# Rests of the first weights: from a subtraction on GpSimd and VectorE to two matmuls and a ScalarE eviction

## The chip, the cores and the metric

The kernel runs on one core of a Trainium2 chip. The metric is device time in microseconds (us) of one execution of the whole program. Five engines work from queues of their own: TensorE (PE in the profile; PEld is its weight load), VectorE (DVE), ScalarE (ACT), GpSimd (POOL) and SyncE (SP), which here only issues DMAs. TensorE writes to PSUM, eight banks of 128 x 512 float32; VectorE and ScalarE read PSUM, GpSimd does not in this kernel.

## The reference

Three steps on 4 x 768 tokens of 8 heads x 48 = 384 features, all float32:

```
for t in range(768):                        # linear attention with decay, state 48 x 48 per head
    cur   = u*k[t] outer v[t]
    y[t]  = r[t] @ (state + cur)
    state = w[t]*state + k[t] outer v[t]
h   = max(y @ w1, y @ w2, y @ w3)           # 384 -> 768, three products, elementwise maximum
x   = h @ w_out                             # 768 -> 384
g   = x @ w_in;  g = g - tanh(g)            # 384 -> 2048
out = g @ w_out2                            # 2048 -> 384
```

The weights arrive as float64 bits, two int32 words per number. The kernel turns each into float32 itself and then splits it into a high part `hi` (the number rounded to the fp32r kind that TensorE multiplies in one pass) and a rest `lo = g - hi`, also fp32r.

## The kernel before

**Products.** Every product of the two feed-forward layers is made of three fp32r matmuls (`mm3`, lines 438 to 441): weight `hi` by activation `hi` (L439), weight `lo` by activation `hi` (L440), weight `hi` by activation `lo` (L441), summed in one PSUM bank of 512 columns.

**Stages.** The 24 chunks of 128 tokens are taken in six groups of four. A prologue computes the attention of chunks 0 to 3. Then comes one pass per group: 18 slots (six blocks `f` of 128 hidden features, three products each, nine matmuls per slot), then three output tiles `d` of 18 matmuls with `WOh`/`WOl`. During the slots of a group the attention of the next group is woven in: `advance(slot)` (L606) issues its steps, twenty for four chunks. After group 5 comes the second layer (`h_unit`, `o_unit`), which the change leaves alone.

**Conversion of the first weights.** The weights of the first layer are 24 units of 128 x 384: units 0 to 17 are the slots' weights in order, units 18 to 23 those of the output tiles, two for each. `w1_unit` (L482) converts one with `conv` (L431): ScalarE takes the high word (L64), VectorE makes the float32 bits in four instructions (L70 to L73), ScalarE rounds to `hi` (L435), and GpSimd subtracts to `lo` (L436); for the four units in `LO_DVE` VectorE subtracts. `g` lies in a ring `cv` of five tiles. Each unit's raw bits are loaded on SyncE's queue eight units ahead.

**When units are issued.** The prologue issues 0, 1, 3 and 4 of them after chunks 0, 1, 2 and 3 (`PRO`), so units 0 to 7. In group 0, `w1_upto(slot + 4 + max(0, slot - 8))` at the end of a slot issues unit 8 after slot 5, one unit after each of slots 6, 7 and 8, and two after each of slots 9 to 14. So unit 23 is issued after slot 14.

**Banks.** `mm` is a ring over banks 0 to 3 that runs on through all groups. A slot's bank is read out by ScalarE (L624, first product) or VectorE (L626, maximum with the others); an output tile's by ScalarE (L650). Banks 4 and 5 hold attention scores (with 0 and 1 in the prologue), 6 and 7 attention outputs and small sums. `h_unit` takes banks 0 and 1 in turn.

**Order.** Tiles and semaphores are the framework's: it takes the program's order as priority and lays down one fixed order per engine. So instructions of two units, or of a slot and the attention, stand interleaved on an engine, and on the chip each engine runs its list strictly as laid down.

Of the kernel before, what the change touches and what calls it, by code (L numbers as in the profile page):

```python
# [10 lines left out]
F32R = mybir.dt.float32r  # L11
# [4 lines left out]
ALU = mybir.AluOpType  # L16
# [3 lines left out]
P = 128  # L20
# [13 lines left out]
EARLY_B = 6  # L34
BONUS_DVE = [0, 1, 2, 4]
VALS_DVE = [5]
LO_DVE = [12, 15, 18, 21]
EARLY_R = [0, 5]
W2A = 12
MM_BANKS = [0, 1, 2, 3]  # L40
# [8 lines left out]
UN = KT * P  # L49
# [13 lines left out]
def abs_f64(act, raw, out):  # L63
    act.activation(out, raw[:, 1::2].bitcast(F32), AF.Abs)  # L64


def bits_f64(dve, raw, out):
    oi = out.bitcast(I32)
    high, low = raw[:, 1::2], raw[:, 0::2]
    dve.tensor_scalar(out, out, bits_f32(LO_BITS), bits_f32(HI_BITS), ALU.max, ALU.min)  # L70
    dve.tensor_scalar(oi, oi, 3, 0x3FFFFFFF, ALU.logical_shift_left, ALU.bitwise_and)  # L71
    dve.scalar_tensor_tensor(oi, high, -0x40000000, oi, ALU.bitwise_and, ALU.bitwise_or)  # L72
    dve.scalar_tensor_tensor(oi, low, 29, oi, ALU.logical_shift_right, ALU.bitwise_or)  # L73
# [16 lines left out]
def main_path(ctx, tc, wT, rkT, w0, rk0, nat, vpad, uT, ub, wA, wo1, wi2, wo2, outT, count):  # L90
    nc = tc.nc
    pe, act, dve, pool, sp = nc.tensor, nc.scalar, nc.vector, nc.gpsimd, nc.sync

    def pool_(name, side="left"):
        return tc.tile_pool(name=name, bufs=1, side=side, reuse_waits="tile")

    const = ctx.enter_context(pool_("const"))
# [11 lines left out]
    bank = [pm.tile([P, 512], F32, name=f"bank{i}") for i in range(8)]  # L109
# [9 lines left out]
    mm = Ring([bank[i] for i in MM_BANKS])  # L119
    scb = Ring([bank[4], bank[5], bank[0], bank[1]])  # L120
    yab, dsb = bank[6], bank[7]

    ident = const.tile([P, P], F32, name="ident")
    dmask = const.tile([P, C], U8, name="dmask")
    ubt = const.tile([P, DM], F32, name="ubt")
    sq = const.tile([P, 2 * NCH], F32, name="sq")
# [37 lines left out]
    def ys(d, g):  # L164
        c = g * 512
        return Y[:, d, c:c + 512] if c < YA else Yb[0][:, d, c - YA:c - YA + 512]
# [207 lines left out]
    def att_steps(c, col):  # L374
        n = c + 1 if c + 1 < NCH else None
        st = {}

        def k0():
            scores(c, st)
            masked(c, st)  # L380
            if n and n < EARLY_B:
                bonus(n)
            if n:
                scans(n)

        def k1():
            if c < EARLY:
                key_turn_pe(c)
            if c >= EARLY_B:
                diagonal(c)  # L390
            if n:
                decays(n)
                if n >= EARLY_B:
                    bonus(n)
                squares(n)

        def k2():
            state_mm(c)
            state_add(c)
            if n:  # L400
                if n >= EARLY:
                    key_turn(n)
                    key_order(n)
                state_decay(n)

        def k3():
            if n:
                bonus_sum(n)

        def k4():  # L410
            outputs(c)
            outputs_out(c, col)
            if n and n < EARLY_B:
                bonus_vals(n)
            load_next(c)

        return [k0, k1, k2, k3, k4]

    def in_range():

        dve.tensor_scalar(sq, sq, 1.0, None, ALU.is_lt)
        dve.tensor_reduce(okp, sq, AX.X, ALU.min)
        pe.matmul(dsb[0:1, 0:1], okp, ones, start=True, stop=True)
        dve.tensor_copy(count, dsb[0:1, 0:1])


    def w1_upto(n):
        while w1n < min(n, 24):
            w1_unit()

    def conv(raw, hi, lo, eng=pool):  # L431
        g = cv()
        abs_f64(act, raw, g)
        bits_f64(dve, raw, g)
        act.copy(hi, g)  # L435
        eng.tensor_tensor(lo, g, hi, ALU.subtract)  # L436

    def mm3(bk, wh, wl, ah, al, first, last):
        pe.matmul(bk, wh, ah, start=first, stop=False)  # L439
# [11 lines left out]
    def warm(n):  # L451

        for _ in range(n):
            pe.matmul(bank[3], zeros[:, 0:P], zeros, start=True, stop=True)

    zeros = xs[:, KT - 1, 256:512].bitcast(BF16)
    pool.memset(zeros, 0.0)
# [9 lines left out]
    act.activation(okp, ones, AF.Square)  # L467
    make_identity(nc, ident)
    pool.tensor_copy(dmask, ident)

    Yi = Y.rearrange("p a b -> p (a b)").bitcast(I32)
    w1raw = [wA[:, i // 3, i % 3 * UN:(i % 3 + 1) * UN] for i in range(3 * F1)]
    w1raw += [wo1[:, i * UN:(i + 1) * UN] for i in range(2 * KT)]

    def w1_load(i):
        sp.dma_start(Yi[:, (i % SLOTS) * 2 * UN:(i % SLOTS + 1) * 2 * UN], w1raw[i].bitcast(I32))

    WAf = [t.rearrange("p f j k m -> p (f j k m)") for t in (WAh, WAl)]
    WOf = [t.rearrange("p d f m -> p (d f m)") for t in (WOh, WOl)]
    w1n = 0  # L480

    def w1_unit():  # L482
        nonlocal w1n
        i = w1n
        w1n += 1
        o = i % SLOTS * 2 * UN
        t, q = (WAf, i) if i < 3 * F1 else (WOf, i - 3 * F1)
        conv(Yi[:, o:o + 2 * UN], t[0][:, q * UN:(q + 1) * UN], t[1][:, q * UN:(q + 1) * UN], dve if i in LO_DVE else pool)
        if i + SLOTS < len(w1raw):
            w1_load(i + SLOTS)  # L490

# [53 lines left out]
    def w2_pump():  # L545
        while free and fetch:
            kind, f = fetch.pop(0)
            staged[kind, f] = free.pop(0)
            sp.dma_start(staged[kind, f], (wi2, wo2)[kind][:, f].bitcast(I32))

    def w2_queue(units):
        todo.extend(units)
        fetch.extend(units)
        w2_pump()
# [23 lines left out]

    c0 = 0
    for g, gn in enumerate(GROUPS):  # L580
        n = gn * C
        lastg = g == len(GROUPS) - 1
        nchunks = [] if lastg else list(range(c0 + gn, c0 + gn + GROUPS[g + 1]))
        steps = [s for i, c in enumerate(nchunks) for s in att_steps(c, i * C)]
        nslots = 3 * F1
        if g == len(GROUPS) - 2:
            def w2_open():
                nonlocal W2a
                in_range()
                p_att.close()  # L590
                p_third.close()
                yb = ctx.enter_context(pool_("yb", "right"))
                Yb.append(yb.tile([P, KT, NT - YA], F32, name="Yb"))
                w2p = ctx.enter_context(pool_("w2p", "right"))
                W2a = [w2p.tile([P, W2A, UN], F32R, name=f"W2{x}a") for x in "hl"]
                free.extend(w2p.tile([P, 2 * UN], I32, name=f"w2st{i}") for i in range(2))
                w2_queue([(0, f) for f in range(W2A)])

            steps += [w2_open, None] + [w2_step] * 6
        if lastg:  # L600
            free.extend([xsi[:, 0:2 * UN], xsi[:, 2 * UN:4 * UN]])
            w2_pump()
            steps = [w2_step] * W2A
        done = 0

        def advance(slot):  # L606
            nonlocal done
            want = min(len(steps), -(-len(steps) * (slot + 1) // nslots))
            while done < want:
                if steps[done]:  # L610
                    steps[done]()
                done += 1
            if g == 0:
                w1_upto(slot + 1 + LEAD + max(0, slot - 8))

        slot = 0
        for f in range(F1):
            for j in range(3):
                bk = mm()
                for k in range(KT):  # L620
                    mm3(bk[:, 0:n], WAh[:, f, j, k], WAl[:, f, j, k], xh[:, k, 0:n], xl[:, k, 0:n], k == 0, k == KT - 1)
                if j == 0:
                    t = tmp()
                    act.copy(t[:, 0:n], bk[:, 0:n])  # L624
                else:
                    dve.tensor_tensor(t[:, 0:n], bk[:, 0:n], t[:, 0:n], ALU.max)  # L626
                if j == 2:
                    act.copy(hh[:, f, 0:n], t[:, 0:n])  # L628
                    (dve if f == F1 - 1 else pool).tensor_tensor(hl[:, f, 0:n], t[:, 0:n], hh[:, f, 0:n], ALU.subtract)  # L629
                advance(slot)  # L630
                slot += 1
        if lastg:
            assert not todo
            p_wA.close()
            wo2p = ctx.enter_context(pool_("wo2p"))
            WO2 = [wo2p.tile([P, F2, UN], F32R, name=f"WO2{x}") for x in "hl"]
            units = [(1, f) for f in range(F2)]
            for i, f in enumerate(range(W2A, F2)):
                units.insert(3 * i + 4, (0, f))
            w2_queue(units)  # L640
        for d in range(KT):
            bk = mm()
            for f in range(F1):
                mm3(bk[:, 0:n], WOh[:, d, f], WOl[:, d, f], hh[:, f, 0:n], hl[:, f, 0:n], f == 0, f == F1 - 1)
            if lastg:
                y_split(0, d)
                w2_step()
            elif d == 0:
                x_split(GROUPS[g + 1] * C)
            act.copy(ys(d, g), bk[:, 0:n])  # L650
        c0 += gn
# [238 lines left out]
```

## Time and profile before

| | |
|---|---|
| median of 3 runs | 881.76 us (880.70 to 886.29) |
| profiled execution | 882.44 us, of which the span of its instructions is 880.7 us |
| TensorE (PE) busy | 839.4 us (95% of the span) |
| VectorE (DVE) busy | 514.6 us (58%) |
| ScalarE (ACT) busy | 335.8 us (38%) |
| GpSimd (POOL) busy | 211.3 us (24%) |
| mean granted TensorE clock | 0.977 of full speed |

Times in the profile count from the span's start. Busy shares of the whole span are means over stages: the prologue (to 55 us), group 0 (to 147 us), groups 1 to 5 (to 463 us) and the second layer each have their own limit. A matmul's printed duration overlaps the next one's, so the pace of matmuls is read from start to start.

### The profile page before, as it was taken

To read this page: it belongs to the slowest core of one execution; us is meant where nothing else is said; L and a number is where in the kernel's file an instruction comes from. 1 tells how busy PE (TensorE), PEld (TensorE's weight loads), DVE (VectorE), ACT (ScalarE), POOL (GpSimd) and SP (SyncE) were. 2 spreads that over 40 slices of the span, in tenths; PEclk is the share of its full clock that TensorE was granted. 3 is DMA by queue.
4 is the path that set the end of the run, shared out by engine and by line. 5 is a ranking of instruction groups with operands and counts; after the bars stand their busy time and mean duration, and the time that the engine had idled before them with its cause. 6 is when DMAs were issued, how large, how long until landed. Compare 5 with 4: busy or idle time off the path is not lost.

```text
span 880.7 us, 12116 instructions
## 1 busy us (share of the span) xinstructions
PE 839.4 (95%) x4546; PEld 663.7 (75%) x4546; DVE 514.6 (58%) x823; ACT 335.8 (38%) x657; POOL 211.3 (24%) x214
## 2 busy tenths in 40 slices
PE   7789498999999999999998999999999999999996
PEld 5768376777777777788876688888888888888885
DVE  8989976774664764738989734334334334333332
ACT  4644434243234243335455433224223224222332
POOL 6665543542343442420253300000000000000000
PEclk8979799999999999999999999999999999999999
DMA  8744353354244253315534100000000000001001
GB/s 265 220 140 123 90 150 87 106 151 118 68 114 137 80 155 106 86 33 154 142 100 131 36 1 36 0 1 37 1 0 36 1 1 36 1 1 36 0 1 39
DMA packets 40561, 66.48 MB, mean 75 GB/s; under 512 B 6256, under 2 KB 21360, under 8 KB 40496
## 3 DMA queue, kind: packets, MB, share of 16 engines
q1 hardware_dynamic: 40496, 65.64, 25.2%
q8 instruction: 37, 0.61, 0.3%
q14 instruction: 28, 0.23, 0.1%
HBM read 53.23 MB, written 8.65 MB: 70 GB/s over the span
## 4 chain that ended last, share of the span: by engine, by line
PE 82%; DVE 10%; DMA 2%; issue 2%; POOL 1%; SPq 1%; ACT 1%; DVEq 0%; ACTq 0%; POOLq 0%
PE bank L439 26%; PE bank L441 25%; PE bank L440 25%; PE bank L347 3%; DVE cv L72 2%; PE bank L278 2%; DVE cv L73 2%; DMA Y<-in_wA 1%; DVE cv L71 1%; PE bank L311 1%; DVE cv L70 1%; DVE fwd L204 1%; DVE suf L202 0%; DMA rk<-in_rkT 0%; DVE hl L670 0%
## 5 line engine op out<-in xcount | busy, mean ns | idle before, releaser
L668 DVE TENSOR_TENSOR tmp<-bank,tmp 128x512 f32<-128x512 f32 x96 | 66.3, 691 | 174.6 <-ACT tmp L667 174.6
L439 PE MATMUL bank<-xh,WAh 128*128 128x512 f32 x324 | 135.5, 418 | 0.0
L441 PE MATMUL bank<-xl,WAh 128*128 128x512 f32 x324 | 130.1, 402 | 0.8 <-DVE xl L367 0.8
L440 PE MATMUL bank<-xh,WAl 128*128 128x512 f32 x324 | 129.8, 401 | 0.0
L667 ACT ACTIVATE tmp<-bank 128x512 f32<-128x512 f32 x96 | 57.4, 598 | 183.0 <-PE bank L441 183.0
L439 PE MATMUL bank<-hh,WO2h 128*128 128x512 f32 x288 | 114.2, 396 | 1.5 <-ACT hh L669 1.4
L441 PE MATMUL bank<-hl,WO2h 128*128 128x512 f32 x288 | 114.3, 397 | 0.4 <-DVE hl L670 0.3
L440 PE MATMUL bank<-hh,WO2l 128*128 128x512 f32 x288 | 113.7, 395 | 0.0
L670 DVE TENSOR_TENSOR hl<-tmp,hh 128x512 fp32r<-128x512 f32 x96 | 66.4, 692 | 58.9 <-PE bank L441 46.8
L669 ACT CAST hh<-tmp 128x512 fp32r<-128x512 f32 x96 | 59.7, 621 | 72.8 <-DVE tmp L668 72.7
L439 PEld LDWEIGHTS bank<-xh,WAh 128*128 128x128 f32 x324 | 61.8, 191 | 18.4 <-issue 2.4
L441 PEld LDWEIGHTS bank<-xl,WAh 128*128 128x128 f32 x324 | 61.8, 191 | 16.5 <-DVE xl L367 1.2
L629 POOL TENSOR_TENSOR hl<-tmp,hh 128x512 fp32r<-128x512 f32 x30 | 46.5, 1550 | 106.5 <-ACT hh L628 106.5
L440 PEld LDWEIGHTS bank<-xh,WAl 128*128 128x128 f32 x324 | 62.1, 192 | 12.7
L441 PEld LDWEIGHTS bank<-hl,WO2h 128*128 128x128 f32 x288 | 54.1, 188 | 15.7 <-DVE hl L670 3.0
L439 PEld LDWEIGHTS bank<-hh,WO2h 128*128 128x128 f32 x288 | 54.1, 188 | 15.6 <-ACT hh L669 3.3
L440 PEld LDWEIGHTS bank<-hh,WO2l 128*128 128x128 f32 x288 | 54.1, 188 | 12.7
L626 DVE TENSOR_TENSOR tmp<-bank,tmp 128x512 f32<-128x512 f32 x72 | 49.0, 680 | 18.6 <-PE bank L441 14.5
L283 DVE COPY_PREDICATED P<-dmask,sd 128x512 f32<-128x512 uint8 x36 | 32.8, 950 | 45.6 <-POOL P L295 45.6
L628 ACT CAST hh<-tmp 128x512 fp32r<-128x512 f32 x36 | 22.4, 621 | 88.2 <-DVE tmp L626 85.3
L439 PE MATMUL bank<-xh,W2ha 128*128 128x512 f32 x108 | 43.3, 401 | 2.8 <-ACT Yb L650 2.8
L439 PE MATMUL bank<-hh,WOh 128*128 128x512 f32 x108 | 43.3, 401 | 0.4 <-ACT hh L628 0.4
(189 smaller groups left out, 1581.8 us busy)
## 6 DMA issues: line engine op xcount, KB each, us to landing
Y<-in_wA SPq DMA_DIRECT2D x18, 384.0 KB, 5.8
nt<-in_nat SPq DMA_DIRECT2D x12, 576.0 KB, 4.9
rk<-in_rkT SPq DMA_DIRECT2D x30, 192.0 KB, 3.4
w2st<-in_wi SPq DMA_DIRECT2D x12, 384.0 KB, 3.6
third<-in_nat SPq DMA_DIRECT2D x7, 576.0 KB, 4.8
kbd<-fwd SPq DMA_DIRECT2D x15, 256.0 KB, 2.1
fwd<-kbd SPq DMA_DIRECT2D x60, 64.0 KB, 2.0
third<-in_rkT SPq DMA_DIRECT2D x16, 192.0 KB, 3.5
```

Of the source, the lines that this page charges most:

```text
L283: dve.copy_predicated(q, dmask[:, None, :].to_broadcast([P, NP, C]), sdt[c % 2][:, j::2, None].to_broadcast([P, NP, C]))
L347: pe.matmul(yab[64 * j:64 * j + HD, p * C:(p + 1) * C], *t(j), start=i == 0, stop=i == len(terms) - 1)
L439: pe.matmul(bk, wh, ah, start=first, stop=False)
L440: pe.matmul(bk, wl, ah, start=False, stop=False)
L441: pe.matmul(bk, wh, al, start=False, stop=last)
L626: dve.tensor_tensor(t[:, 0:n], bk[:, 0:n], t[:, 0:n], ALU.max)
L628: act.copy(hh[:, f, 0:n], t[:, 0:n])
L629: (dve if f == F1 - 1 else pool).tensor_tensor(hl[:, f, 0:n], t[:, 0:n], hh[:, f, 0:n], ALU.subtract)
L667: act.activation(t, bk, AF.Tanh)
L668: dve.tensor_tensor(t, bk, t, ALU.subtract)
L669: act.copy(hh[:, r], t)
L670: dve.tensor_tensor(hl[:, r], t, hh[:, r], ALU.subtract)
```

## The change

The subtraction of the 24 units leaves GpSimd and VectorE. Instead TensorE sums `identity x g` (float32) and `minus identity x hi` (fp32r) into bank 3, and ScalarE copies the sum to `lo`. This is done for unit i when unit i+2 has been issued (`REST_LAG = 2`); the last ones follow unit 23. Bank 3 leaves the `mm` ring in group 0, whose ring is therefore three banks, and the ring is set back to its first bank at the start of every group. The warming matmuls go from bank 3 to bank 2. The conversions of the second layer's weights (`w2_step`) keep their subtractions.

```diff
-LO_DVE = [12, 15, 18, 21]
+REST_LAG = 2
...
+    minus = const.tile([P, P], F32R, name="minus")
...
         act.copy(hi, g)
-        eng.tensor_tensor(lo, g, hi, ALU.subtract)
+        if eng is not pe:
+            eng.tensor_tensor(lo, g, hi, ALU.subtract)
+        return g
+
+    def conv_rest(g, hi, lo):
+
+        pe.matmul(bank[3][:, 0:UN], ident, g, start=True, stop=False)
+        pe.matmul(bank[3][:, 0:UN], minus, hi, start=False, stop=True)
+        act.copy(lo, bank[3][:, 0:UN])
...
-            pe.matmul(bank[3], zeros[:, 0:P], zeros, start=True, stop=True)
+            pe.matmul(bank[2], zeros[:, 0:P], zeros, start=True, stop=True)
...
+    act.mul(minus, ident, -1.0)
...
+    rests = []
...
-        conv(Yi[:, o:o + 2 * UN], t[0][:, q * UN:(q + 1) * UN], t[1][:, q * UN:(q + 1) * UN], dve if i in LO_DVE else pool)
+        hi, lo = (x[:, q * UN:(q + 1) * UN] for x in t)
+        rests.append((conv(Yi[:, o:o + 2 * UN], hi, lo, pe), hi, lo))
+        if len(rests) > REST_LAG or w1n == len(w1raw):
+            conv_rest(*rests.pop(0))
+        if w1n == len(w1raw):
+            while rests:
+                conv_rest(*rests.pop(0))
...
     for g, gn in enumerate(GROUPS):
+        mm.items, mm.i = [bank[i] for i in MM_BANKS[0:3 if g == 0 else 4]], 0
```

## Rows read from the trace of the kernel before

**Rows 1.** Busy time by stretch: us of the stretch, then PE, PEld, DVE, ACT, POOL, clock.

```profile
14.00:55.20 41.20, 32.08 (x268) 28.87 (x268) 39.66 (x62) 24.59 (x66) 26.38 (x28) 0.83 0.74 231
55.20:79.30 24.10, 23.79 (x138) 18.45 (x138) 21.26 (x36) 11.67 (x28) 12.45 (x12) 0.87 0.30 89
79.30:94.90 15.60, 15.59 (x113) 12.19 (x111) 13.70 (x24) 5.33 (x11) 8.97 (x10) 1.00 0.28 87
94.90:107.40 12.50, 0.00 (x0) 0.00 (x0) 12.03 (x19) 6.46 (x13) 6.79 (x7) 0.67 0.33 78
107.40:138.70 31.30, 27.84 (x177) 21.26 (x177) 26.31 (x45) 13.89 (x30) 13.75 (x14) 0.91 0.44 138
138.70:400.00 261.30, 260.29 (x1790) 202.31 (x1791) 158.71 (x240) 97.07 (x200) 101.08 (x109) 1.00 0.37 106
```

**Rows 2.** Timeline of TensorE around its longest wait: start, us, instruction, idle before.

```profile
107.43 0.88 PE L311 MATMUL bank<-nt,kcn 128*48 128x48 f32 x16 [12.54 <-ACT kcn L263]
```

**Rows 3.** Line 436 in three stretches: DVE busy, then POOL busy.

```profile
14.00:55.20 41.20, 0.00 (x0) 10.28 (x7) 0.83 0.74 231
55.20:94.90 39.70, 0.55 (x1) 9.70 (x7) 0.92 0.30 88
94.90:138.70 43.80, 2.26 (x3) 6.54 (x6) 0.84 0.41 121
```

**Rows 4.** Timeline of DVE, ACT and POOL: two conversions, the second beside a GpSimd subtraction.

```profile
99.60 0.56 DVE L72 SCALAR_TENSOR_TENSOR cv<-Y,cv 128x384 int32<-128x384 int32 x1
100.78 0.51 ACT L435 CAST WAh<-cv 128x384 fp32r<-128x384 f32 x1 [1.75 <-DVE cv L73]
101.37 0.99 POOL L436 TENSOR_TENSOR WAl<-cv,WAh 128x384 fp32r<-128x384 f32 x1 [2.92 <-ACT WAh L435]
101.45 1.33 DVE L72 SCALAR_TENSOR_TENSOR cv<-Y,cv 128x384 int32<-128x384 int32 x1
```

**Rows 5.** The same timeline: first and last DVE row lengthened beside line 436.

```profile
17.83 1.98 POOL L436 TENSOR_TENSOR WAl<-cv,WAh 128x384 fp32r<-128x384 f32 x1
18.94 1.43 DVE L216 TENSOR_TENSOR third<-third 128x512 f32<-128x512 f32 x1
...
133.03 1.00 POOL L436 TENSOR_TENSOR WOl<-cv,WOh 128x384 fp32r<-128x384 f32 x1 [4.33 <-ACT WOh L435]
133.20 1.25 DVE L72 SCALAR_TENSOR_TENSOR cv<-Y,cv 128x384 int32<-128x384 int32 x1
```

**Rows 6.** Timeline of TensorE: float32 matmuls of 128 columns, then fp32r at either clock.

```profile
45.88 0.38 PE L334 MATMUL bank<-ident,nt 128*96 128x128 f32 x2
46.10 0.38 PE L335 MATMUL bank<-tmp,nt 128*96 128x128 f32 x2
...
58.10 0.63 PE L440 MATMUL bank<-xh,WAl 128*128 128x512 f32 x1
58.53 0.63 PE L441 MATMUL bank<-xl,WAh 128*128 128x512 f32 x1
...
73.69 0.48 PE L439 MATMUL bank<-xh,WAh 128*128 128x512 f32 x1
74.00 0.39 PE L440 MATMUL bank<-xh,WAl 128*128 128x512 f32 x1
74.24 0.39 PE L441 MATMUL bank<-xl,WAh 128*128 128x512 f32 x1
```

**Rows 7.** Line 352, a ScalarE eviction of 96 x 384: ns min/median/max.

```profile
L352 ACT COPY xs<-bank x5: 462/471/475, 21.2 to 76.9; 96x384 f32<-96x384 f32 x5
```

**Rows 8.** Timeline at the change from group 3 to 4, PE and ACT.

```profile
346.31 0.39 PE L439 MATMUL bank<-xh,WAh 128*128 128x512 f32 x1
...
346.51 0.59 ACT L650 COPY Y<-bank 128x512 f32<-128x512 f32 x1 [1.21 <-PE bank L441]
```

**Rows 9.** Timeline where the second layer starts, PE and ACT.

```profile
468.42 0.80 PE L439 MATMUL bank<-xh,W2ha 128*128 128x512 f32 x1 [2.77 <-ACT Yb L650]
```

## The prediction

> **What bounds the kernel now.** I read the busy times by stretch first, since only the first 139 us hold work that the change touches. From 138.7 us on TensorE is busy 260.29 of 261.30 us [rows 1]: whatever group 0 gains or loses arrives at the end whole. Before that the limit changes hands. To 55.2 us (first matmul of group 0) VectorE is busy 39.66 of 41.20 us: the prologue is VectorE's. From 55.2 to 94.9 TensorE is busy 39.4 of 39.7 us. Then, from 94.9 to 107.4, it does nothing at all while VectorE is busy 12.03 of 12.50 us; and from 107.4 to 138.7 it has 27.84 of 31.30 us, so 3.46 us idle [rows 1]. The timeline shows what the empty stretch is: one attention matmul (L311) waits 12.54 us for ScalarE's copy of the keys, which stands behind roundings that themselves wait for VectorE's conversions [rows 2, 4]; the matmuls of slot 11 stand behind it. So VectorE and TensorE are each the limit for part of the way, and the change takes work from the first and gives work to the second.
>
> **What leaves VectorE and GpSimd.** 20 subtractions of 26.5 us in all go from GpSimd, four of 2.8 us in all from VectorE [rows 3]. GpSimd's own time bounds nothing above; what counts is its neighbour. A conversion's L72 takes 0.56 us alone and 1.33 us when a GpSimd subtraction (0.99 us) starts just before it [rows 4]. In the timeline 18 VectorE rows are lengthened like this beside line 436, the first and last of them shown [rows 5]. Their time over the shortest row of the same form, shared with any other GpSimd instruction they overlap, sums to 10.0 us: 3.9 before 55.2, 4.1 from there to 107.4, 2.1 after. VectorE's own four subtractions are 0.55 us each undisturbed, two before 107.4 and two after. So VectorE is relieved by 3.9 us in the prologue, 5.2 us from there to 107.4, 3.2 us after.
>
> The Trainium skill (GPSIMD Engine Reference, Specifications) says that GpSimd shares its SBUF interfaces with VectorE and contends with VectorE instructions of two SBUF inputs or in a two-port mode. The trace agrees in kind (L72 at 1.33 against 0.56 us). Read at its widest, that all 26.5 us of GpSimd's subtractions come back to VectorE, the rule would take away the 1.9 us of slip below and no more, since TensorE then sets the end: 879 us.
>
> **What TensorE takes on.** A float32 matmul of 128 columns takes 0.22 us from start to start, an fp32r one of 512 columns 0.24 us, the first fp32r after float32 0.31 us [rows 6]. So one rest costs 3 x 0.22 + 0.75 x 0.24 + 0.08 = 0.92 us, an estimate from those rows; no row is of its form. From below, without the change of kind, 0.84; from above, at the lower clock, where the 512 columns take 0.43 us [rows 6], twice the first two terms: 1.7. I take 0.92, since the stretches that matter ran at full clock. By the issue positions unit i's rest follows unit i+2: rests 0 to 5 fall in the prologue, 6 to 13 after slots 5 to 10 (all before 94.9 us), 14 to 23 after slots 11 to 14. The first six are covered by TensorE's idle 9.1 us of the prologue [rows 1] and would cost 5.5 us without it; the next eight meet a TensorE with no room: +7.4 us; the last ten are +9.2 us.
>
> **What ScalarE takes on.** 24 evictions of 384 columns at 0.47 us (the nearest row [rows 7]) make 11.3 us, and one product of 128 columns, earlier. ScalarE is busy 24.59 of 41.20 us in the prologue and half the time later [rows 1], so I cost them at nothing; if each stood in VectorE's chain it would be 2.8 us in the prologue. Behind a late eviction stand the next rounding, attention copies and bank reads. The raw loads on SyncE's queue wait for VectorE's reads as before and are not moved; the renamed warming bank costs nothing, since bank 2 is as empty then as bank 3.
>
> **Less room.** `cv[i]` is now held until rest i, so unit i+5 cannot start before it; and a slot's bank must be read out two slots later instead of three. No row of before shows either wait in this stretch. From below zero; from above 4 us, two undisturbed conversions of 2.0 us (two each of rows like L70 and L72: 2 x 0.35 + 2 x 0.56 = 1.8, and gaps). I take 2.
>
> **The ring set back.** 21 tiles per group on four banks end on bank 0, and the next group now starts on bank 0. At the change from group 3 to 4 the next matmul starts at 346.31 while the last bank is read from 346.51 to 347.10 [rows 8]: on the same bank it would wait 0.8 us. This happens at four changes (groups 1 to 5) and at the second layer's first tile, where already in before the second tile waited 2.77 us for such a read [rows 9]. From below zero (attention scores fill the gap, but for the last two places), from above 4 x 0.8 + 2.8 = 6.0. I take 2.
>
> **The sum.** Group 0 starts 3.5 us earlier (3.9, less what TensorE and ScalarE add). TensorE comes to slot 11's wait at 94.9 - 3.5 + 7.4 = 98.8; VectorE lets go of it at 107.4 - 3.5 - 5.2 = 98.7, with the slip 100.7. So L311 runs 6.7 us earlier, after a wait of 1.9 us instead of 12.5. Some ten matmuls after the wait started at the lower clock, 1.2 GHz (the mean granted clock of the stretch of the wait is 0.67, of the next one 0.91 [rows 1]); at 0.24 instead of 0.43 us that is -1.9. The last ten rests add 9.2 and use up the 3.46 us of idle time: +5.7. Ring: +2. In all -6.7 - 1.9 + 5.7 + 2 = -0.9 us on the profiled execution's 882.44, so 881.5. The median shown is 0.7 us below that execution: **881 us**. What is late next is TensorE itself: the gap that VectorE made is filled with the work that closed it.
>
> **Rivals.**
> *All of it hides, faster.* No slip, rests at 0.84, nothing lost at the ring, and TensorE, kept going by the prologue's rests, starts group 0 at full clock (0.87 mean in the stretch from 55.2 us [rows 1], worth some 2 us). L311 at 98.7: -8.7; -1.9; 8.4 - 3.46 = +4.9; -2: -7.7 us, 874; with the idle time of the prologue's tail gone as well, 872. For it: 16 us of TensorE idle in group 0. Against: eight rests fall where there is none. 0.18.
> *TensorE stands at the rests, slower.* Its list is fixed, so one rest that is not ready holds all matmuls behind it, as the 12.54 us wait did [rows 2]. After each of slots 9 to 14 two or more rests follow each other on the one bank 3: the second needs ScalarE's eviction of the first, and on ScalarE this can stand behind the rounding of the next unit, which waits for a conversion of some 2 us. It decides as soon as that rounding ends after the slot's last matmul; before, the roundings came at 100.78 us [rows 4] for unit 16, where slot 12 would now end at about 101, so it is close. Six places x 2 us = +12 on the sum: 893; half of them 887. Against: the order is laid down with these waits in view, and slots can stand between two rests. 0.20. The Trainium skill (TensorE: Matmul & The Clock Gate, Part 3, The mechanism) says matmuls start and end strictly in order, which the 12.54 us wait bears out.
> *The ring costs its full price.* Six us instead of two: 885. 0.12.
> *The relief does not come.* If GpSimd's other instructions move up into the freed time and lengthen VectorE's rows as the subtractions did, none of the 10.0 us returns, only VectorE's own subtractions. Group 0 then starts 0.4 us later than before, VectorE releases L311 at 107.4 + 0.4 - 1.1 + 2 = 108.7, the low clock stays, and 1.3 + 5.7 + 2 = +9.0: 891; with half of the relief 886. Against: the other GpSimd instructions have their own releasers and are no more in number. 0.08.
> My own case has the remaining 0.42.
>
> **How the numbers follow.** My case alone runs from 877 to 885 (slip 0 to 4, rests at 0.84 to 1.0, ring 0 to 4). The range takes in the faster rival whole, and the slower one but for its full price: 872 to 890. One per cent, 8.8 us, is about what a measurement of this kernel can tell from no change. Faster by over 1% is most of the first rival's lower half with some unforeseen order: 0.13. Slower by over 1% is most of the standing rival and a tail of the last: 0.17. Within: 0.70.
>
> **What would show it.** Right: no GpSimd or VectorE row of the subtraction in the first 140 us; L72 rows near 0.56; 24 evictions near 0.47; rests near 0.92 from start to start; the wait at L311 under 4 us; TensorE's busy share near full from 55 us to the end of group 0; group 1 starting within 3 us of where it did. Wrong: waits of TensorE for an eviction of bank 3 or a rounding, of more than 6 us in all (standing rival); group 0 ending over 6 us earlier (first rival); waits for L650 at the starts of groups 2 to 5 of near 0.8 us each (ring); VectorE rows in the prologue as long as before (no relief).

## The result

The changed kernel takes 887.83 us (median of 20 runs, 884.73 to 891.72) against 883.69 us for the kernel before in the same study (20 runs, 880.70 to 886.56): a ratio of 1.0057, 95% interval [1.0046, 1.0068]. The medians differ by 4.1 us, the ratio puts it at 5.0 us slower (4.1 to 6.0). I had forecast 0.9 us faster. The time lies in the range and inside the one per cent that the prediction called no change, but the sign was wrong by more than the interval. The profiled execution took 887.88 us, its span 886.2 us (before: 880.7), its mean granted clock was 0.987 (before: 0.977). TensorE is busy 856.3 us (97%), 16.9 us more; VectorE 503.7, 10.9 less; ScalarE 344.3, 8.5 more; GpSimd 190.5, 20.8 less. One of the twelve runs of e12 below fell in a slow state (1030.27 us at a mean granted clock of 0.748) and is left out of its ratio.

**Where the time went.** In the profile group 0 starts 2.8 us earlier (52.43 instead of 55.21), is 6.7 us longer (to 151.03 instead of 147.09), groups 1 to 5 lose nothing more (315.88 us instead of 316.36), and the second layer from its first matmul to the end is 2.0 us longer. In sum +5.4 us of span.

Busy time by stretch of group 0, from its first matmul to the first of group 1: the kernel before, then the one after; columns as in [rows 1]. The second row of each cuts it at the matmul that waited 12.54 us [rows 2].

```profile
55.21:147.09 91.88, 75.57 (x462) 58.24 (x461) 78.43 (x127) 39.37 (x85) 45.28 (x42) 0.89 0.36 105
107.43:147.09 39.66, 36.20 (x213) 27.61 (x213) 31.42 (x51) 15.90 (x34) 17.07 (x16) 0.93 0.42 131
```

```profile
52.43:151.03 98.60, 91.87 (x520) 67.35 (x520) 75.99 (x126) 49.38 (x112) 34.78 (x32) 0.97 0.41 129
99.28:151.03 51.75, 48.20 (x261) 34.76 (x261) 38.07 (x69) 27.98 (x63) 16.92 (x16) 1.00 0.45 141
135.80:400.00 264.20, 263.88 (x1831) 205.22 (x1830) 154.10 (x232) 95.89 (x197) 96.77 (x106) 1.00 0.35 100
```

The length less PE's busy time is what TensorE stood: 16.3 us before, 6.7 after. So 9.6 us of standing went and 16.3 us of work came. The last row answers to the last of [rows 1]: TensorE is full from there on.

The gap itself is closed. The timeline of TensorE after, where [rows 2] had the wait, shows the same 16 attention matmuls with none:

```profile
98.96 0.39 PE L448 MATMUL bank<-xh,WAh 128*128 128x512 f32 x1
99.28 0.57 PE L312 MATMUL bank<-nt,kcn 128*48 128x48 f32 x16
99.77 0.73 PE L448 MATMUL bank<-xh,WAh 128*128 128x512 f32 x2
```

In its place the waits of TensorE in group 0 of the kernel after (line that waits, releaser; us in all, times, longest) are these:

```profile
PE bank L443 <- ACT WOl L445: 1.9, 2, 1.3
PE bank L449 <- ACT WAl L445: 1.8, 1, 1.8
PE bank L228 <- issue: 1.3, 1, 1.3
PE bank L443 <- ACT WAl L445: 0.9, 1, 0.9
PE bank L348 <- DVE P L284: 0.7, 1, 0.7
```

4.6 of these 6.6 us are waits for L445, the eviction of a rest. How the longest comes about is read from the timeline of TensorE, ScalarE, VectorE and GpSimd from 79 to 86 us:

```profile
81.33 0.81 PE L443 MATMUL bank<-cv,ident 128*128 128x384 f32 x2
81.68 0.63 PE L444 MATMUL bank<-WAh,minus 128*128 128x384 f32 x1
...
85.16 0.67 PE L449 MATMUL bank<-xh,WAl 128*128 128x512 f32 x1 [1.83 <-ACT WAl L445]
85.62 0.63 PE L450 MATMUL bank<-xl,WAh 128*128 128x512 f32 x1
86.05 0.63 PE L448 MATMUL bank<-xh,WAh 128*128 128x512 f32 x1
...
83.30 0.51 ACT L436 CAST WAh<-cv 128x384 fp32r<-128x384 f32 x1 [4.06 <-DVE cv L73]
83.71 0.58 ACT L642 COPY tmp<-bank 128x512 f32<-128x512 f32 x1
84.19 0.54 ACT L64 ACTIVATE cv<-Y 128x384 f32<-128x384 f32 x1
84.63 0.47 ACT L445 CAST WAl<-bank 128x384 fp32r<-128x384 f32 x1
...
79.25 1.44 DVE L71 TENSOR_SCALAR cv<-cv 128x384 int32<-128x384 int32 x1
80.73 1.26 DVE L72 SCALAR_TENSOR_TENSOR cv<-Y,cv 128x384 int32<-128x384 int32 x1
82.02 1.24 DVE L73 SCALAR_TENSOR_TENSOR cv<-Y,cv 128x384 int32<-128x384 int32 x1
...
85.16 0.36 DVE L71 TENSOR_SCALAR cv<-cv 128x384 int32<-128x384 int32 x1
85.56 0.56 DVE L72 SCALAR_TENSOR_TENSOR cv<-Y,cv 128x384 int32<-128x384 int32 x1
86.15 0.56 DVE L73 SCALAR_TENSOR_TENSOR cv<-Y,cv 128x384 int32<-128x384 int32 x1
...
78.94 1.54 POOL L647 TENSOR_TENSOR hl<-tmp,hh 128x512 fp32r<-128x512 f32 x1 [2.15 <-ACT hh L646]
80.44 1.12 POOL L220 TENSOR_TENSOR nt<-nt,ubt 128x384 f32<-128x384 f32 x1
81.64 1.20 POOL L221 TENSOR_TENSOR nt<-nt 128x384 f32<-128x384 f32 x1
```

Read from the bottom: three GpSimd instructions that were there before lie beside a conversion, whose rows take 1.44, 1.26 and 1.24 us (0.36, 0.56 and 0.56 in the next unit, from 85.16 on). ScalarE's rounding stands 4.06 us for it, and behind the rounding, in ScalarE's fixed list, stand two more instructions (L642, L64) and then the eviction of a rest that TensorE had finished near 82.2. A matmul with that `lo` waits 1.83 us, and the matmuls after it run at 0.43 us from start to start, the lower clock (granted clock 0.79 from 84 to 92 us). The Trainium skill (TensorE: Matmul & The Clock Gate, Part 3, The mechanism) says that matmuls start and end strictly in order; the rows agree, since everything behind 85.16 stood with it.

**VectorE.** Busy time on the ring `cv` from 55.2 to 138.7 us (column DVE), before and after: the conversions, and before also VectorE's own four subtractions.

```profile
55.20:138.70 83.50, 41.31 (x70) 0.88 0.35 105
```

```profile
55.20:138.70 83.50, 34.55 (x63) 0.96 0.39 123
```

From 14 to 166 us the two sums are 62.10 and 53.16 us. The relief is there. Half of the 24 L72 rows take 0.56 us or less after; before, their median was 0.87 us.

### The profile page after: what moved, and what is told of

It is laid out like the page before. It is cut to its first block, busy times and chain, and to the rows that moved or that the text cites. A ratio compares the mean times of both kernels' runs of the same rounds, so it can differ in the third digit from the quotient of the medians.

```text
span 886.2 us, 12252 instructions
## 1 busy us (share of the span) xinstructions
PE 856.3 (97%) x4618; PEld 673.4 (76%) x4618; DVE 503.7 (57%) x819; ACT 344.3 (39%) x682; POOL 190.5 (21%) x194
## 4 chain that ended last, share of the span: by engine, by line
PE 81%; DVE 11%; issue 3%; ACT 2%; DMA 1%; POOL 1%; SPq 1%; DVEq 0%; ACTq 0%
PE bank L448 25%; PE bank L450 24%; PE bank L449 24%; PE bank L348 4%; PE bank L279 2%; DVE cv L73 2%; DVE cv L72 2%; DVE cv L70 1%; DVE cv L71 1%; PE bank L312 1%; DVE fwd L205 1%; POOL WO2l L438 1%; DVE suf L203 1%; DMA kbd<-fwd 1%; DVE rk L212 1%
## 5 line engine op out<-in xcount | busy, mean ns | idle before, releaser
L647 POOL TENSOR_TENSOR hl<-tmp,hh 128x512 fp32r<-128x512 f32 x30 | 48.5, 1616 | 130.5 <-ACT hh L646 130.5
L644 DVE TENSOR_TENSOR tmp<-bank,tmp 128x512 f32<-128x512 f32 x72 | 49.0, 681 | 17.5 <-PE bank L450 16.9
L284 DVE COPY_PREDICATED P<-dmask,sd 128x512 f32<-128x512 uint8 x36 | 30.7, 903 | 45.0 <-POOL P L296 45.0
L449 PE MATMUL bank<-xh,W2la 128*128 128x512 f32 x108 | 43.8, 406 | 0.0
```

Of the source, the lines that this page charges most:

```text
L284: dve.copy_predicated(q, dmask[:, None, :].to_broadcast([P, NP, C]), sdt[c % 2][:, j::2, None].to_broadcast([P, NP, C]))
L449: pe.matmul(bk, wl, ah, start=False, stop=False)
```

## Experiments

Each ratio is to the kernel before in the same job; its median there was 883.45 us in e1 to e4, 882.57 in e5 to e8, 883.59 in e9 to e12. Four theories stand in the expectations. **P**: the rests cost TensorE's own time. **S**: they cost standing. **R**: the ring set back costs something of its own. **V**: units held back by `cv` leave VectorE late.

**e1, the ring continued.** The edit in the kernel after:

```diff
-        mm.items, mm.i = [bank[i] for i in MM_BANKS[0:3 if g == 0 else 4]], 0
+        mm.items, mm.i = [bank[i] for i in MM_BANKS[0:3 if g == 0 else 4]], g
```

> The changed kernel, with the bank ring of groups 1 to 5 started where the kernel before had it (group g at bank g mod 4) instead of at bank 0; group 0 is untouched. Theory R (the reset makes the last output tile of group 5 share bank 0 with the first tile of the second layer): some 2 us of the 5.5 us come back, 0.2% of the time, and the order of the first tiles of the second layer is that of before; the ratio to before goes from 1.0057 to 1.0035. Rival (all of the loss sits in group 0, and the later growth is chance): no change, 1.0055.

885.06 us (12 runs), ratio 1.0015 [0.9999, 1.0031]. That is 0.42% or 3.7 us less than the kernel after, so R holds, with more than the 2 us that its forecast gave it. Where it lies is seen where the second layer starts, TensorE of the kernel after, then of e1:

```profile
467.60 0.39 PE L448 MATMUL bank<-xh,W2ha 128*128 128x512 f32 x1
471.89 0.80 PE L448 MATMUL bank<-xh,W2ha 128*128 128x512 f32 x1 [3.91 <-ACT Yb L668]
472.48 0.63 PE L449 MATMUL bank<-xh,W2la 128*128 128x512 f32 x1
```

```profile
468.51 0.39 PE L450 MATMUL bank<-xl,W2ha 128*128 128x512 f32 x1
471.68 0.50 PE L448 MATMUL bank<-xh,W2ha 128*128 128x512 f32 x1 [2.78 <-ACT Yb L668]
```

With the reset, bank 0 holds the last output tile, and the matmul that stands for its eviction (L668) is reached after four matmuls instead of nine. From the second layer's first matmul to the end of the span it is 419.2 us after and 417.6 in e1. At the changes of groups, where the prediction feared 0.8 us four times, no wait of the kind exists. Groups 1 to 5 are 1.4 us longer than in e1 all the same, with no wait to show for it. In the profiles of all these kernels this stretch takes 314.3 to 317.9 us, so one profile of each cannot price it; where the rest of the 3.7 us lies stays open.

**e8, the reset alone.** The kernel before with one line:

```diff
+        mm.i = 0
```

> The kernel before with one line added: the ring of four banks set back to bank 0 at each group; conversions, subtractions and group 0 unchanged. Theory R (the reset costs what e1 gave back): 886 to 888 against 883.5, the second layer's first tile waiting over 3 us on the eviction of its bank. Without R: 883 to 884.5, and e1's gain was something else of the order.

884.88 us (12 runs), ratio 1.0021 [1.0005, 1.0037]: 1.9 us (0.4 to 3.3). The tile waits 3.89 us for its eviction, as after. R holds at the size that the prediction took, though below the 886 to 888 us that R's expectation asked for. In its profile the second layer is 0.9 us longer than before, so the wait there accounts for part of the 1.9 us. That the reset costs more together with the rests (3.7 us) than alone (1.9) is not shown, since the intervals overlap.

**e3, no rests.** e1 without them; the product of `lo` is made with `hi`, so the output lacks the rest (the two matmul calls are not shown):

```diff
-            conv_rest(*rests.pop(0))
-        if w1n == len(w1raw):
-            while rests:
-                conv_rest(*rests.pop(0))
+            rests.pop(0)
...
```

> The changed kernel without rests: no lo is made for the first weights (neither subtraction nor matmuls nor evictions), and their second matmul takes hi in its place, so the output differs; bank ring as in e1_phase, three banks in group 0. It shows what the relief of VectorE alone is worth. Prediction's sum: start of group 0 3.5 us earlier, L311 released 5.2 us earlier still, then 3.2: 8 to 12 us faster than before, ratio 0.987 to 0.991. Rival (VectorE's time moves to contention with other GpSimd instructions, or TensorE binds anyway): 3 to 5 us, 0.995.

872.72 us (5 runs), ratio 0.9867 [0.9846, 0.9889]: the relief alone is worth 11.8 us. Against e1 the rests cost 1.0015 - 0.9867 = 1.5%, 13 us. The two nearly cancel; with the 3.7 us of the reset they make up the 5 us of the change. The relief alone does not close the gap: here the attention matmul of [rows 2] still waits, and the rests fill that wait. The profiled run took 878.25 us, 5.5 above the median of the five, so its windows serve for the kind of a wait more than for its size.

```profile
101.44 0.88 PE L312 MATMUL bank<-nt,kcn 128*48 128x48 f32 x16 [6.57 <-ACT kcn L264]
```

**e9, rests without the relief.** e1 with GpSimd's subtraction beside them:

```diff
-        if eng is not pe:
-            eng.tensor_tensor(lo, g, hi, ALU.subtract)
+        (pool if eng is pe else eng).tensor_tensor(lo, g, hi, ALU.subtract)
```

> e1 with GpSimd's subtraction kept beside every rest (lo is written twice, first by GpSimd for all 24 units, then by the rest): the rests without the relief. Theory P (rests 13 us, relief 12 us, both real and independent): e1 + 8 to 12 = 893 to 897, the rows L72 of VectorE lengthened again to 1 us and more. If the relief were not real, that is if e3 gained because nothing waited for lo any more: 884 to 888.

898.75 us (5 runs), ratio 1.0170 [1.0147, 1.0193]: 13.7 us over e1, more than the 8 to 12 expected, so the subtractions do cost time of this size, and e3's gain was not just that nothing waited for `lo`. The run is not a clean counterpart of the relief: GpSimd subtracts all 24 units here, not 20, and TensorE waits 2.9 us for L437 itself in group 0. VectorE on `cv` is long again, 38.30 us from 55.2 to 138.7 (e1: 36.25), and 61.39 us from 14 to 166 (e1: 53.68):

```profile
55.20:138.70 83.50, 38.30 (x61) 0.90 0.41 129
```

The Trainium skill (GPSIMD Engine Reference, Specifications) says that GpSimd contends with VectorE instructions of two SBUF inputs for shared interfaces; the runs agree, and price it here at 7.7 us of VectorE's time (61.39 less 53.68) for 24 subtractions. The prediction's last rival, that the relief does not come, is out.

**e5, short rests.** e1 with the float32 product cut to 32 columns, so that `lo` lacks most of `g`; waits, bank and eviction stay:

```diff
-        pe.matmul(bank[3][:, 0:UN], ident, g, start=True, stop=False)
-        pe.matmul(bank[3][:, 0:UN], minus, hi, start=False, stop=True)
+        pe.matmul(bank[3][:, 0:32], ident, g[:, 0:32], start=True, stop=True)
+        pe.matmul(bank[3][:, 0:UN], minus, hi, start=True, stop=True)
```

> The kernel after with the banks continued as in e1, but each rest multiplies only 32 of the 384 float32 columns (its lo is wrong, the output differs); the waits of the rest, the hold on cv, bank 3 and the eviction stay. A rest then takes some 0.35 us instead of 0.9, an estimate from 0.06 + 0.18 + the change of kind. Theory P (the price of the rests is TensorE's own time): 19 rests x 0.55 = 10.5 us of group 0, most of it returned: 874 to 877 against e1's 885.1, group 0 near 88 us. Theory S (the price is the standing at the rests: evictions of bank 3, cv held): what is taken from the matmuls comes back as waits, group 0 stays over 94 us, 882 to 885, with idle time in group 0 over 12 us.

873.43 us (6 runs), ratio 0.9881 [0.9856, 0.9906], 11.8 us under e1. Group 0 in e1, then in e5:

```profile
55.15:152.21 97.06, 90.34 (x520) 66.05 (x520) 75.94 (x126) 49.04 (x112) 35.78 (x32) 0.98 0.41 131
```

```profile
54.26:140.72 86.46, 81.82 (x515) 63.21 (x515) 74.46 (x127) 50.12 (x114) 35.64 (x30) 0.98 0.43 138
```

Of the 10.6 us by which it is shorter, 8.5 are TensorE's busy time and 2.1 standing (97.06 - 90.34 = 6.7 to 86.46 - 81.82 = 4.6). P holds. Its standing is now mostly for VectorE (first row below), where e1's was for evictions: 4.5 us for L445 in e1, 0.9 here. So with shorter rests the waits for evictions went and waits for conversions came in their place.

```profile
PE bank L443 <- DVE cv L73: 2.8, 3, 1.5
PE bank L443 <- ACT WOl L445: 0.4, 1, 0.4
```

**e7, no lag.** e1 with

```diff
-REST_LAG = 2
+REST_LAG = 0
```

> As e1, but each rest follows its own unit at once (lag 0 instead of 2), so cv is held less and the rest waits for its own rounding. Theory P: no change from e1, 884 to 887, as TensorE's time is the same. Theory S, cv held the cause: idle of ScalarE before the conversion falls, group 0 shorter by 3 us: 881 to 883. Theory S, TensorE standing at a rest that is not ready the cause: it stands longer, 888 to 893.

883.97 us (12 runs), ratio 1.0009 [0.9993, 1.0025], not to be told from e1. In group 0 TensorE stands 6.8 us for L445 in six places (e1: 4.5 in four). Group 0 starts at 59.87 and is 91.80 us long, so the 5.3 us by which it is shorter than in e1 come after a start that is 4.7 us later. The profiled run was 2.7 us above the median. P's forecast holds; neither form of S decides.

**e2, seven `cv` buffers**, the two more taken from one raw slot (the kernel after, seven raw slots instead of eight):

```diff
-SLOTS = 8
+SLOTS = 7
...
-        g = cv()
+        g = (cvw if eng is pe else cv)()
...
+    Yf = Y.rearrange("p a b -> p (a b)")
+    cvw = Ring(cv.items + [Yf[:, i * UN:(i + 1) * UN] for i in range(2 * SLOTS, 16)])
```

> The changed kernel with seven conversion buffers instead of five for the first weights; the two more lie in what was the eighth raw slot, so raw loads run seven units ahead instead of eight. Theory V (buffers held until the rest starve VectorE, and TensorE then waits for it and drops to the lower clock): the waits of ScalarE's L64 for TensorE go, TensorE's 6.6 us of idle time and some 3.7 us of lower clock in group 0 shrink by half or more: 4 to 6 us faster than the changed kernel, ratio to before 0.999 to 1.001. Theory P (19 rests of 0.9 us simply fill TensorE's list in group 0): under 1 us, 1.005.

888.63 us (6 runs), ratio 1.0060 [1.0042, 1.0077]: V is not borne out. Group 0 is 3 us shorter than after and starts 4.4 us later (56.79). Whether the later start comes from the slot it gave up was not tried.

**e11, three banks** in group 0, the kernel before else:

```diff
+        mm.items, mm.i = [bank[i] for i in MM_BANKS[0:3 if g == 0 else 4]], g
```

> The kernel before with three banks instead of four in group 0, the ring else continued; nothing else changed. Theory P: TensorE gave its banks back in time with three, so at most 1 us: 882.5 to 884. Theory S: part of the standing is the bank, 885 to 888, and waits of the first layer's matmuls on L646 in group 0.

883.50 us (12 runs), ratio 1.0007 [0.9988, 1.0025]. Three banks cost nothing that shows; a first-layer matmul waits 2.4 us for L627 in a group that has 15.7 us of standing anyway.

**e4, e6, e10 and e12: only some of the units.** The others are subtracted as before; the set is the edit: units 0 to 7 (with four banks throughout), 0 to 13, 14 to 23, and 0 to 5 with 18 to 23. Shown is the form of the last two, from the kernel after, without the lines on when a rest follows; the first two have a bound in place of the set. All but the first have three banks in group 0 and e1's ring.

```diff
+        g = conv(Yi[:, o:o + 2 * UN], hi, lo, pe if i in REST_PE else dve if i in LO_DVE else pool)
+        if i in REST_PE:
+            rests.append((g, hi, lo))
...
```

> The kernel before, with rests on TensorE for units 0 to 7 alone, all of them summed within the prologue; units 8 to 23 subtract on GpSimd and VectorE as before, four banks everywhere, no reset. Theory P: group 0 starts 2.8 us earlier as in the changed kernel and then runs as before: 2 to 3 us faster than before, ratio 0.997. Rival (VectorE sets the wait of TensorE in group 0, so what starts earlier waits longer): within 1 us, 1.000.

882.23 us (12 runs), ratio 0.9986 [0.9972, 1.0001]: 1.2 us, between P's 2 to 3 and the rival's one, and the interval reaches into both. Three of the eight rests fall in group 0, not in the prologue, and group 0 starts 1.9 us earlier. The wait of [rows 2] is 3.5 us here, and the next of its kind 6.8 us (before: 1.3).

> Rests on TensorE for units 0 to 13 only; the last ten units are subtracted as before (GpSimd, VectorE for three), banks continued as in e1, three banks in group 0. Theory P: the first 14 rests cost TensorE 7.4 us before a gap that VectorE made and give VectorE back up to 8 us; the last ten, 9.2 us for 3.2 us of relief, are not paid: 875 to 879 against 883.5 of before. Theory S: standing at bank 3 and at cv takes it back: 882 to 886.

883.66 us (12 runs), ratio 1.0014 [0.9996, 1.0032]. P's forecast missed by 5 us or more. The gap at 107 us is gone here too; TensorE reaches the output tiles at 128.11 us (before 131.07, after 138.28) and then stands, as its waits in group 0 show:

```profile
PE bank L450 <- ACT hh L647: 3.5, 1, 3.5
PE bank L452 <- DVE hl L648: 3.1, 1, 3.1
PE bank L451 <- ACT WAl L447: 1.8, 1, 1.8
```

VectorE, busy 79.13 of the group's 97.42 us, is late with the last conversions, and `hh` and `hl` stand behind them. The gap was moved, not closed.

> Rests on TensorE for the last ten units only (14 to 23), the first 14 as in the kernel before (GpSimd, VectorE for unit 12), banks continued, three banks in group 0. Theory P with the two limits in turn: the gap before 107 us stays near 12 us, ten rests cost 9 us of a stretch with 3.5 us of idle time, so 886 to 889 against 882.6 of before. If the late rests are the good half, since e6 lost its gain at VectorE behind the last conversions: 879 to 882.

885.46 us (12 runs), ratio 1.0024 [1.0008, 1.0039]. The wait of [rows 2] is there at 7.2 us, and ten rests (9.0 us) replace only part of the standing. P had asked for 3.4 to 6.4 us over before; the medians differ by 1.9.

> A try at beating both: rests on TensorE for units 0 to 5, which fall in the prologue, and 18 to 23, where e6 showed VectorE late again; units 6 to 17 as in the kernel before, banks continued, three banks in group 0. Theory P: group 0 starts 2 to 3 us earlier for nothing, the middle is as before, the last six rests cost 5.4 us against 3.5 us of idle time and some 2 us of VectorE's: 879 to 882. Theory S: 884 to 888.

882.54 us (12 runs), ratio 0.9992 [0.9976, 1.0009]. Both forecasts missed (879 to 882, 884 to 888), P's by half a microsecond. No set beats the kernel before by more than its interval.

**The rate of exchange.** Group 0 in all these profiles, from the windows (standing is length less PE's busy time; rests are those inside group 0; e1 repeats the program of after in this group):

| | rests | length | PE busy | standing | VectorE busy |
|---|---|---|---|---|---|
| before | 0 | 91.88 | 75.57 | 16.3 | 78.43 |
| e4 | 3 | 91.77 | 78.64 | 13.1 | 82.22 |
| e12 | 7 | 92.95 | 80.00 | 13.0 | 78.75 |
| e6 | 9 | 97.42 | 85.29 | 12.1 | 79.13 |
| e10 | 10 | 93.52 | 81.76 | 11.8 | 75.01 |
| after | 19 | 98.60 | 91.87 | 6.7 | 75.99 |
| e1 | 19 | 97.06 | 90.34 | 6.7 | 75.94 |
| e5, short rests | 19 | 86.46 | 81.82 | 4.6 | 74.46 |
| e3, none | 0 | 84.71 | 75.59 | 9.1 | 69.80 |

A rest takes some 0.9 us of TensorE's time from start to start, and about half a microsecond of standing goes for each one in group 0: 3.3 us for 7, 4.2 for 9, 4.5 for 10, 9.6 for 19. That is not a price per unit. All but e10 have five more rests in the prologue, which relieve VectorE too; counted over all units that changed (8, 12, 14, 10 and 24 from e4 to after) it is 0.3 to 0.45 us each. Each row of the table is one profile, and PE's busy time also holds the low clock, which differs: it grows by 0.6 to 1.1 us per rest. e3's row is from a run 5.5 us above its median. More of the relief may lie in the start of group 0, but its time in one profile scatters too much to price it: after and e1 have the same program up to there and start it at 52.43 and 55.15. Six profiles with rests in the prologue (after, e1, e4, e5, e6, e12) start it at 52.4 to 55.2 us, four with the old subtractions there (before, e8, e10, e11) at 55.0 to 56.5.

## Why the prediction was wrong

- **What bounds the kernel** [rows 1, 2]: right. The gap was VectorE's: relieving VectorE alone gains 11.8 us (e3) and shortens the wait.
- **The relief.** On `cv` it is 8.9 us (62.10 to 53.16, own subtractions included). The prediction's 10.0 + 2.8 counted other rows beside the subtractions too, so the two are not quite the same thing; with no rests the same view has 50.92. Rows that other GpSimd work lengthens, as at 79 to 83 us, are among what stayed; how much they come to was not summed.
- **The wait at L311**: predicted 6.7 us earlier with 1.9 us left. Measured 8.2 us earlier (99.28) with none. That is in part a matter of order: 11 fewer first-layer matmuls stand ahead of it than before, and six rests of group 0 instead of the eight that the prediction put there. They come behind it: 13 rests, where the prediction counted ten.
- **The price of a rest** (0.92 us): right. From start to start 0.81 us at its best (76.96 to 77.77), 0.90 in the mean over group 0 (17.2 us for 19; one more than predicted falls there, from 53.18 on).
- **The standing that is left: this step failed.** The prediction kept 1.9 us of slip and let the last ten rests use up the 3.46 us after the gap: 14.1 us of standing were to go. 9.6 went. From L312 to group 1 TensorE's standing is 51.75 - 48.20 = 3.55 us, as much as before (39.66 - 36.20 = 3.46), though 13 rests lie there; 2.8 us of it are waits of a rest for the eviction of the one before on bank 3, 0.7 for `P`. The sum priced `lo`'s way through ScalarE at nothing because ScalarE is idle half the time; in ScalarE's fixed list an eviction stood behind a rounding that waited for VectorE (4.06 us before 83.30, the eviction at 84.63), with the engine busy only 39% of the span. The prediction had this as its standing rival, at 6 or 12 us, and decided against it; it came at 4.6 us, under the 6 us that it had named as the sign. Group 1 starts 3.9 us later than before, where the prediction asked for within 3. That an earlier eviction would win the 4.6 us back is not shown: no run moved it in ScalarE's list or to another engine, and in e5, where these waits are down to 0.9 us, waits for conversions came instead.
- **The low clock** (-1.9): the feed-forward and attention matmuls of group 0 took 0.9 us less in all, from start to start (91.87 less 17.2 against 75.57). The old stretch of low clock went, new ones came behind the waits at 63.34 and 85.16.
- **The ring** (+2): 1.9 us alone (e8), 3.7 with the rests (e1 against after). A longer wait shows at the second layer's first tile and none at the changes of groups, so the size was right, or somewhat small, for half the reasons given.
- **Less room**: three banks cost nothing (e11). `cv` held does make ScalarE's L64 stand for L443 (6.3 us before 140 us), but neither more buffers (e2) nor less lag (e7) brings a gain.
- **In numbers**, on the profiled execution: standing 4.5 us more than forecast, low clock 1.0 more, rests 0.6 more, start of group 0 0.7 less gained; the second layer cost the 2 us forecast. -0.9 becomes some +6; the span shows +5.4, the interval 4.1 to 6.0. The medians say the same without a profile: relief and rests together were forecast at -2.9 us and measured +1.3 (e1, interval -0.1 to 2.7), a miss of 4.2, and the ring 3.7 instead of 2.

## What to carry to other kernels

Work moved from a late engine to a full one pays only by the standing that it removes, and one gap is not that figure: VectorE was busy for 78 of the 92 us of group 0, longer than TensorE (76), and where its gap at 107 us closed, other waits followed (e6: for `hh` and `hl`; after: for L445). Price such a move as an exchange, time added per unit against standing removed per unit, and test the two halves apart, one kernel with the relief and without the new work (e3), one with the new work and without the relief (e9). And an eviction on an engine with room can cost what it stands behind, so look at what waits ahead of it in that engine's list.

## What the runs showed of the hardware

- A three-instruction rest, 384 columns of float32 and 384 of fp32r, takes TensorE 0.81 us from start to start at the full clock. Cutting the float32 part from 384 to 32 columns took 8.5 us from 19 rests, 0.45 us each.
- Waits of nearly the same length were followed by a lower clock in one run and not in another: after 1.35 us at 63.34 in the kernel after the stretch from 55 to 75 us has a granted clock of 0.91, after 1.36 us at 66.08 in e1 it has 1.00 (the two rows below, in this order). These two traces give no rule for the clock after a wait of that size.

```profile
55.00:75.00 20.00, 18.65 (x126) 15.08 (x125) 19.00 (x27) 8.83 (x23) 9.83 (x9) 0.91 0.27 85
55.00:75.00 20.00, 18.64 (x122) 14.78 (x122) 18.97 (x28) 10.93 (x29) 11.56 (x10) 1.00 0.40 130
```

- A conversion's rows are long beside other elementwise instructions of GpSimd too (L647, L220, L221), not beside the subtraction alone: 1.44 instead of 0.36 us, and 1.26 and 1.24 instead of 0.56 us.
